# Sparse attention and expert layer on one core: second operands of VectorE in PSUM, splits of the last weights on ScalarE and VectorE, a new order

## The chip, the core and the metric

The kernel runs on one core of a Trainium2 chip. A core has five engines with instruction queues of their own: TensorE (PE, matmuls, into PSUM), VectorE (DVE), ScalarE (ACT), GpSimd (POOL) and SyncE (SP, which issues transfers). The program is one launch. The metric is the device time of that launch in microseconds, as the median of several runs. A profile is one further execution, recorded by the hardware profiler.

## The reference

The input is `q`, `k`, `v` of 8 batches, 8 heads, 576 rows and 64 features, all float32, and the weights of an expert layer.

```python
# attention: keep the scores that lie within tau of their row's maximum
scores = q @ k.T / sqrt(64)
scores = where(scores >= max(scores) - tau, scores, -1e9)
p = exp(scores - max(scores)); p /= sum(p) + 1e-9
x = (p @ v)  ->  4608 tokens of 512 features (8 heads side by side)
# expert layer: each token goes to one of 8 experts
logits = x @ w_gate + modality_bias[modality_id]
e = argmax(logits); gate = softmax(logits)[e]
out = gate * (relu(x @ w1[e]) @ w2[e])      # w1 512x1024, w2 1024x512
```

## The kernel before

**Attention.** 8 batches have 4 pairs of heads each, a pair has 9 steps of 128 score rows, 288 steps in all. A step is: PE writes 128 x 576 scores into a pair of PSUM banks (`qk`, L827); DVE takes the row maximum (`nm`, L836 and L838); ACT the exponential (`e`, L842); DVE masks and sums the row (`pr`, L854); PE transposes `pr` (L880), ACT copies the result out (L883), and PE multiplies it by `v` (L761). Since float32 products are made of rounded parts, each matmul operand is kept as a high part and the rest (`hi`, `lo`), and a product takes three matmuls. For keys and queries POOL makes these parts (`stack`, L727 and L729).

**Routing.** After the fourth pair of a batch PE computes the gate's logits (`gate`), and `route` (L990) runs on DVE: logits summed over heads (L996), their maximum (L997), its subtraction (L998), the first expert that reaches it (L1001 to L1004), a count by matmuls of how many earlier tokens each expert has (`f3`), and the place of each token in the expert's list (L1020 to L1024). `pos` keeps the running count. POOL scatters the tokens' numbers and row factors into a table in HBM (`tab`). The modality bias is prepared once on DVE (`late_constants`, L644 to L652).

**Slots.** An expert's work is done in slots of 256 to 512 tokens of one expert (`slot`, L1131). SP reads the expert and place from an integer in SBUF, loads the table's rows (`tb`) and 16 weight tiles of 256 KB (`wload`, into `raw`), POOL gathers the tokens (`xg`), `xt` scales each by its row factors (`xn`, L1182), PE transposes it, ACT and DVE make `xh` and `xl`; `wsplit` makes the two parts of each weight tile (L1219 or L1221 the high one, L1223 the low one); `l1` is the first layer (L1239, then `hh` on ACT, `hl` on DVE), `l2` the second (L1271, then `y`), and POOL writes the rows to the output with an indirect transfer (L1290). Eight side slots run beside attention or just behind it: after some batches are routed, `pick` (L1042) takes the expert with enough tokens waiting. In them the scaling and both parts of the weights are POOL's work. When all batches are routed, `pick_rest` (L1058) makes the list of the slots that are left from the counts, in some 40 small DVE instructions on one partition; three such slots are always run (`last_slot`: two of 512, one of 320 tokens; further ones under a condition). In these the scaling, the high parts (ACT) and the low parts of `w1` (DVE) are not on POOL, the low parts of `w2` are. Tiles of the last slots have names with a `t` ahead (`tw1h`, `txg`).

**The order.** Nothing is issued in the order of the text. Each step is an `op` with an engine, an assumed duration, what it reads and writes, and a due time. `SHIFTS` is a compressed table with one byte for each op that moves its due time by up to 8 us. `Plan.order` (L148) plays the engines forward with these durations: an engine that is free takes the ready op that is due first; PSUM banks are given out on the way. While attention runs, two pairs of banks belong to scores and four single banks (`bk`) to all else; afterwards all eight are single (`pm` are the four former ones). An op that names a `Group` holds its bank from its first to its last op. What comes out is the fixed order of every engine's queue. Lines of `late_constants`, `route`, `pick_rest` and `slot` are those that the change edits, beside the planner's constants.

Of the kernel before, what the change touches and what calls it, by code (L numbers as in the profile page):

```python
# [77 lines left out]
class Plan:  # L78
# [4 lines left out]
    LAND = (0.2, 1.05, 1.7, 4.5)  # L83
# [62 lines left out]
    def order(self, banks, late):  # L146
# [54 lines left out]
        def begin(e, t):  # L201
# [51 lines left out]
            for j in o.succ:  # L253
                x = ops[j]
                same = x.eng == o.eng and o.dma is None
                x.soon = max(x.soon, fin + (self.NEXT if same else self.LAT).get(o.eng, 0.0 if same else 0.04))
                x.left -= 1
                if not x.left and x.hot:
                    coming.add(j)
# [7 lines left out]
        while heap:  # L267
            t = heap[0][0]
            while heap and heap[0][0] <= t + 1e-9:
# [9 lines left out]
                else:  # L279
# [10 lines left out]
                    for j in o.succ:  # L290
                        s = ops[j]
                        same = s.eng == o.eng and o.dma is None
                        s.ready = max(s.ready, t + (self.NEXT if same else self.LAT).get(o.eng, 0.0 if same else 0.04))
# [52 lines left out]
def tile_attn_moe(  # L346
# [166 lines left out]
    pos2 = tiles(glob, 2, [P, NT + 1, NE], F32, "pos")  # L513
# [104 lines left out]
    def late_constants():  # L618
# [24 lines left out]
        def f():  # L643
            nc.vector.tensor_copy(out=mid_f[:, 1, :], in_=mid_i.rearrange("p b t two -> p (b t) two")[:, :, 0])  # L644
            nc.vector.tensor_scalar(out=mid_f[:, 0, :], in0=mid_f[:, 1, :], scalar1=0.0, scalar2=None,
                                    op0=ALU.is_equal)
        op("DVE", 0.8, f, [(bi, b) for b in range(B + 1)], [bf])
# [4 lines left out]
        op("DVE", 0.45, lambda: nc.vector.tensor_tensor(out=bias_t, in0=bias_t, in1=bias_u, op=ALU.add),  # L652
# [286 lines left out]
    def x_out(p):  # L939
# [6 lines left out]
        for a in range(KC):  # L946
# [3 lines left out]
                 src.rearrange("i k p r -> i k (p r)"), rd=[src], wr=[("xs", b, h, a)], us=0.6)  # L950
# [36 lines left out]
    def counted(nb):  # L987
        return pos2[(nb - 1) % 2][:, NT, :] if nb else creg

    def route(b):  # L990
# [3 lines left out]

        def f1():
            V.tensor_reduce(out=lt, in_=lg.rearrange("p c h e -> p c e h"), axis=AX.X, op=ALU.add)  # L996
            V.tensor_reduce(out=mx, in_=lt, axis=AX.X, op=ALU.max)  # L997
            V.tensor_tensor(out=lt, in0=lt, in1=mx.unsqueeze(2).to_broadcast(shp_t), op=ALU.subtract)  # L998

        def f2():  # L1000
            V.scalar_tensor_tensor(out=fe, in0=lt, scalar=0.0, in1=iota_m.unsqueeze(1).to_broadcast(shp_t),  # L1001
                                   op0=ALU.is_ge, op1=ALU.mult)
            V.tensor_reduce(out=mn, in_=fe, axis=AX.X, op=ALU.min)
            V.tensor_tensor(out=oh[:, 0:NT, :], in0=iota_x, in1=mn.unsqueeze(2).to_broadcast(shp_t), op=ALU.is_equal)  # L1004
        op("DVE", 1.35, f1, [lg], [lt, mx])
# [12 lines left out]
        def f4():  # L1018
            rkv = g.t[:, 0:(NT + 1) * NE].rearrange("p (t e) -> p t e", e=NE)
# [5 lines left out]
        op("DVE", 1.0, f4, [g, counted(b), oh], [pos, posf, posi])  # L1025
# [32 lines left out]
    def pick_rest():  # L1058
        left = fin["pool"].tile([1, NE], F32, name="left", bufs=1)
        nc.vector.tensor_tensor(out=left, in0=counted(B)[0:1, :], in1=nxt, op=ALU.subtract)  # L1060
        done = fin["pool"].tile([1, NE], F32, name="done", bufs=1)
        nc.vector.tensor_tensor(out=done, in0=nxt, in1=creg[0:1, :], op=ALU.subtract)
# [3 lines left out]
        for z, w in enumerate((WM, WH, 0)):  # L1066
# [4 lines left out]
        nc.vector.tensor_reduce(out=cnt[:, 1:4, :], in_=th, axis=AX.X, op=ALU.add)  # L1071

        ns = fin["pool"].tile([1, 3, NE], F32, name="ns", bufs=1)
        nc.vector.tensor_tensor(out=ns, in0=cnt[:, 1:4, :], in1=cnt[:, 0:3, :], op=ALU.subtract)
        off = fin["pool"].tile([1, 3, NE], F32, name="off", bufs=1)
        nc.vector.scalar_tensor_tensor(out=off, in0=done.unsqueeze(1).to_broadcast([1, 3, NE]),
                                       scalar=1.0 / W, in1=cnt[:, 0:3, :], op0=ALU.mult, op1=ALU.add)
        yield
        cum = fin["pool"].tile([1, 3, NE], F32, name="cum", bufs=1)
# [6 lines left out]
        nc.vector.tensor_tensor(out=off, in0=off, in1=cum, op=ALU.subtract)  # L1086
# [6 lines left out]
        ej = fin["pool"].tile([1, 3, MAXC], F32, name="ej", bufs=1)  # L1093
# [3 lines left out]
        em = fin["pool"].tile([1, 3, MAXC], F32, name="em", bufs=1)  # L1097
        nc.vector.tensor_scalar(out=em, in0=ej, scalar1=float(-NE), scalar2=None, op0=ALU.add)
        for z in range(3):
            nc.vector.tensor_tensor(out=le[:, z], in0=em[:, z].unsqueeze(2).to_broadcast(SHP),  # L1100
                                    in1=iota_m[0:1, :].unsqueeze(1).to_broadcast(SHP), op=ALU.is_equal)
            nc.vector.tensor_tensor(out=le[:, z], in0=le[:, z], in1=off[:, z:z + 1, :].to_broadcast(SHP),
                                    op=ALU.mult)
            yield
        bj = fin["pool"].tile([1, 3, MAXC], F32, name="bj", bufs=1)
# [3 lines left out]
        nc.vector.tensor_scalar(out=bj, in0=bj, scalar1=float(W), scalar2=float(W), op0=ALU.mult, op1=ALU.add)  # L1109
        nc.vector.scalar_tensor_tensor(out=bj, in0=ej, scalar=float(CAP), in1=bj, op0=ALU.mult, op1=ALU.add)  # L1110
# [19 lines left out]

    def slot(z, where, nrow, WT, rg, xt_eng, keys, late=(), hold=()):  # L1131
# [3 lines left out]
        c1 = 0.695 * WT / 512 if WT > 256 else 0.36  # L1135
# [5 lines left out]
        def expert():  # L1141
            def f():
                box["e"] = nc.values_load(where()[0], engines=[ET.SP], min_val=0, max_val=NE - 1)
            op("SP", 0.4, f, keys, [(z, "e")])

        def rows():
# [7 lines left out]
            op("SP", 0.9, f, keys + ["tab"] + [("tab", b, t) for b in range(nb) for t in range(NT)], [tb], dma=0.4)  # L1154

        def gather(t):
            def f():
# [7 lines left out]
                   [xg], dma=1.0)  # L1165
            return f

        def xt(t):
            def f():
# [27 lines left out]
        def wload(which, f_):  # L1197
            def f():
# [12 lines left out]
                op("SP", 0.42, g, late + [(z, "e")], [raw], dma=0.9)  # L1211
            return f

        def wsplit(which, f_):
            def f():
                raw = box.pop(("raw", which, f_))
                hi, lo = rg[f"w{which}h"].next(), rg[f"w{which}l"].next()
                if xt_eng:
# [3 lines left out]
                d = xt_eng and which == 1  # L1222
# [36 lines left out]
        def l2(gg, t, y):  # L1259
            def f():  # L1260
# [12 lines left out]
                op("PE", 0.695, h, [wh, wl] + [(x, i) for x in (hh, hl) for i in range(2)], [g])  # L1273
# [98 lines left out]
    for z, (w, nb) in enumerate(SIDE):  # L1372
# [11 lines left out]
        for t, f in slot(z, lambda cells=cells: cells["c"], nb * S, w, rings, False, [pk_i[z]], hold=hold)(t0, span, OPEN):  # L1384
# [13 lines left out]
    def finish():  # L1398
# [4 lines left out]
        steps = pick_rest()  # L1403
        for us in [0.6] + [0.7] * 3 + [0.8] + [0.6] * 3 + [0.9, 0.5, 0.9, 0.6, 0.6, 0.9, 0.7, 1.4, 0.7]:
            op("DVE", us, lambda: next(steps, None), ["fin", counted(B)[0:1], nxt, creg, cnt], [cnt, "si"])
# [28 lines left out]
    def idle(g, n):  # L1434
# [4 lines left out]
        c-k#iXCM^(1OA;&lvFaRH+d<QRgtnIA-i(6oITEV&Yowl<Lu+?jLx3fl7vzyTS}CfS=Qa}|9<#CAD)lTr)McYNexQ&vBBHo{d4OHHd=Oe&n%  # L1439
# [123 lines left out]
```

## Time and profile before

| | |
|---|---|
| median of 3 runs | 995.2 us (991.33 to 996.54) |
| profiled execution | 1002.75 us |
| its span, first to last instruction | 1000.9 us |
| mean granted TensorE clock | 0.988 of full |
| busy: PE, DVE, ACT, POOL | 961.2, 747.2, 614.3, 593.8 us |
| transferred | 159.6 MB, mean 159 GB/s |

Busy times are sums over an engine's instructions without overlaps; register, wait and transfer-issuing instructions are not in them. Starts of matmuls are recorded, their ends are modelled, so back-to-back matmuls overlap in the record. In the profile a line such as L1223 is the kernel's line that issued the instruction. Attention takes the first 770 us or so, the last slots end the program.

### The profile page before, as it was taken

What the parts mean: (1) busy time and instruction counts of PE and PEld (TensorE: products, weight loads), DVE (VectorE), ACT (ScalarE), POOL (GpSimd) and SP (SyncE); (2) the same over time, 40 slices, a digit from 0 to 9 for tenths busy, and PEclk for the clock granted to TensorE, in tenths of its full rate; (3) what the DMA queues carried; (4) which work ended last, traced back from release to release, by engine and by line L of the source; (5) the groups of instructions that cost most, each with busy time, mean ns of one, the idle gap of its engine ahead of it and who ended that gap; (6) DMA issues with size and microseconds to landing.
All of it is one profiled execution on the core that took longest, in us unless ns stands there. A gap on an engine that the chain in (4) does not pass through costs nothing.

```text
span 1000.9 us, 19578 instructions
## 1 busy us (share of the span) xinstructions
PE 961.2 (96%) x6304; PEld 768.8 (77%) x6304; DVE 747.2 (75%) x1792; ACT 614.3 (61%) x1256; POOL 593.8 (59%) x746
## 2 busy tenths in 40 slices
PE   7999999989999999999899999999999989899997
PEld 6776677768787877778789778877887866688886
DVE  6898888878788979878878888879785574625242
ACT  6777678667767776767577668766764233143431
POOL 3533686487378645737667575538964879823241
PEclk9999999999999999999999999999999989999999
DMA  7888989888879996897679786778753376333410
GB/s 162 167 192 183 196 189 191 169 204 185 182 140 194 191 193 128 185 183 167 148 158 200 178 171 147 179 142 186 190 136 87 97 199 200 116 104 103 142 63 28
DMA packets 310448, 159.58 MB, mean 159 GB/s; under 512 B 235902, under 2 KB 281982, under 8 KB 308416
## 3 DMA queue, kind: packets, MB, share of 16 engines
q1 hardware_dynamic: 301024, 138.64, 64.3%
q0 software_dynamic: 7200, 19.07, 6.2%
q8 instruction: 52, 0.85, 0.4%
q10 hardware_dynamic: 2112, 0.52, 0.2%
q14 instruction: 60, 0.49, 0.2%
HBM read 85.98 MB, written 20.73 MB: 107 GB/s over the span
## 4 chain that ended last, share of the span: by engine, by line
PE 48%; DVE 5%; issue 3%; POOL 2%; ACT 1%; another core or an unknown queue 0%; POOLq 0%; ACTq 0%; DVEq 0%
PE bk L1239 11%; PE bk L1271 11%; PE bk L761 7%; PE s L827 7%; PE bk L880 5%; PE pm L1271 3%; PE pm L1239 1%; PE bk L1187 1%; DVE pr L854 1%; DVE nm L836 1%; DVE xn L1182 1%; DVE le L1090 1%; PE bk L893 1%; POOL out_dram L1290 0%; PE bk L961 0%
## 5 line engine op out<-in xcount | busy, mean ns | idle before, releaser
L842 ACT ACTIVATE e<-s,nm 128x576 f32<-128x576 f32 x288 | 213.9, 746 | 73.6 <-DVE nm L836 67.9
L854 DVE SCALAR_TENSOR_TENSOR pr<-s,nm,e 128x576 f32<-128x576 f32 x288 | 231.3, 812 | 28.8 <-ACT e L842 10.2
L836 DVE TENSOR_REDUCE nm<-s 128x1 f32<-128x576 f32 x288 | 214.8, 749 | 30.7 <-PE s L827 25.3
L827 PE MATMUL s<-km,q 128*128 128x288 f32 x1024 | 190.9, 313 | 7.0 <-DVE pr L854 5.0
L883 ACT COPY ptm<-bk 128x512 f32<-128x512 f32 x256 | 146.3, 592 | 45.3 <-PE bk L880 37.0
L827 PEld LDWEIGHTS s<-km,q 128*128 128x128 f32 x1024 | 147.5, 189 | 34.4 <-DVE pr L854 14.0
L880 PE MATMUL bk<-ident,pr 128*128 128x128 f32 x1152 | 166.4, 275 | 1.4 <-DVE hl L1253 1.4
L880 PEld LDWEIGHTS bk<-ident,pr 128*128 128x128 f32 x1152 | 136.6, 141 | 19.1 <-issue 2.9
L761 PE MATMUL bk<-ptm,v_m 128*64 128x256 f32 (+1 forms) x1024 | 139.7, 417 | 2.3 <-ACT ptr L900 2.3
L761 PEld LDWEIGHTS bk<-ptm,v_m 128*64 128x64 f32 x1024 | 69.2, 138 | 53.6 <-issue 11.1
L1253 DVE SCALAR_TENSOR_TENSOR hl<-bk,hh 128x512 fp32r<-128x512 f32 (+3 forms) x78 | 45.9, 591 | 64.3 <-ACT hh L1251 64.1
L1239 PE MATMUL bk<-xh,w1h 128*128 128x512 f32 (+2 forms) x240 | 89.7, 374 | 0.2
L729 POOL TENSOR_TENSOR q<-kqt,q 128x576 fp32r<-128x576 f32 x62 | 88.0, 1423 | 2.3
L1271 PE MATMUL bk<-w2h,hh 128*128 128x512 f32 x200 | 84.7, 423 | 0.0
L1239 PE MATMUL bk<-xh,w1l 128*128 128x512 f32 (+2 forms) x240 | 83.8, 349 | 0.4 <-POOL w1l L1223 0.4
L1223 POOL TENSOR_TENSOR w1l<-raw,w1h 128x512 fp32r<-128x512 f32 x64 | 82.3, 1288 | 2.9
L1239 PE MATMUL bk<-xl,w1h 128*128 128x512 f32 (+2 forms) x240 | 83.6, 348 | 0.0
L1223 POOL TENSOR_TENSOR w2l<-raw,w2h 128x512 fp32r<-128x512 f32 x64 | 81.9, 1284 | 2.2
L1271 PE MATMUL bk<-w2l,hh 128*128 128x512 f32 x200 | 79.5, 398 | 2.0 <-POOL w2l L1223 2.0
L727 POOL CAST q<-kqt 128x576 fp32r<-128x576 f32 x62 | 41.0, 668 | 65.0 <-PE s L827 36.7
L1271 PE MATMUL bk<-w2h,hl 128*128 128x512 f32 x200 | 79.1, 396 | 0.0
L1290 POOL DMA_INDIRECT out_dram<-y,tb x37 | 38.2, 1034 | 61.8 <-DVE y L1283 46.1
(226 smaller groups left out, 1784.7 us busy)
## 6 DMA issues: line engine op xcount, KB each, us to landing
raw<-in_moe_w_dram SPq DMA_DIRECT2D x128, 256.0 KB
km<-q SPq DMA_DIRECT2D x60, 288.0 KB
q<-q SPq DMA_DIRECT2D x30, 576.0 KB
nk<-km SPq DMA_DIRECT2D x97, 144.0 KB
traw<-in_moe_w_dram SPq DMA_DIRECT2D x48, 256.0 KB
xs<-xq SPq DMA_DIRECT2D x64, 144.0 KB
v_m<-in_v_dram SPq DMA_DIRECT2D x64, 128.0 KB
kq<-in_q_dram SPq DMA_DIRECT2D x46, 144.0 KB
```

What stands on the lines that cost most here:

```text
L729: op("POOL", 1.425, lambda s=s: nc.gpsimd.tensor_tensor(out=q2[:, 1, s], in0=kqt[:, s], in1=f32(q2[:, 0, s]), op=ALU.subtract), [kqt[:, s] ...
L761: nc.tensor.matmul(out=o, lhsT=lhsT, rhs=rhs, start=start, stop=stop, skip_group_check=True)
L827: nc.tensor.matmul(out=g.t[:, hf, 0:SH], lhsT=a, rhs=x, start=(z == 0), stop=(z == len(passes) - 1))
L836: op("DVE", 0.757, lambda: nc.vector.tensor_reduce(out=nm[:, 0, x:x + 1], in_=g.t[:, :, 0:SH], axis=AX.XY, op=ALU.max, negate=True), [g], ...
L842: op("ACT", 0.747, lambda: nc.scalar.activation(out=e, in_=g.t[:, :, 0:SH], func=AF.Exp, bias=nm[:, 0, x:x + 1]), [g, nm[:, 0, x:x + 1]], ...
L854: op("DVE", 0.826, lambda: nc.vector.scalar_tensor_tensor(out=pr.rearrange("p (a x) -> p a x", a=2), in0=g.t[:, :, 0:SH], scalar=nm[:, 1, ...
L880: op("PE", 0.44, lambda: [nc.tensor.transpose(out=g.t[:, kc * P:(kc + 1) * P], in_=pr[:, kc * P:(kc + 1) * P], identity=ident) for kc in r ...
L883: op("ACT", 0.583, lambda: nc.scalar.copy(out=o, in_=g.t.rearrange("a (k p) -> a k p", p=P)), [g], [o])
L1223: op("DVE" if d else "POOL", 0.686 if d else 1.29, lambda: (nc.vector if d else nc.gpsimd).tensor_tensor(out=lo.t, in0=raw.t, in1=f32(hi.t ...
L1239: nc.tensor.matmul(out=g.t[:, 0:WT], lhsT=a.t[:, cs], rhs=x.t[:, c, 0:WT], start=(c == 0 and y == 0), stop=(c == KC - 1 and y == 2))
L1253: op("DVE", 0.1 + 0.58 * WT / 512, lambda: nc.vector.scalar_tensor_tensor(out=hl.t[:, 0:WT], in0=g.t[:, 0:WT], scalar=0.0, in1=f32(hh.t[:, ...
L1271: nc.tensor.matmul(out=g.t, lhsT=a.t[:, ts], rhs=w.t, start=(y == 0 and i == 0), stop=(y == F2 - 1 and i == 2))
```

## The change

1. In `route` the intermediate results (maximum, its comparison, the expert's number, the positions) lie in the PSUM bank that holds the count, in place of SBUF tiles; it is opened by the first instruction. One `is_ge` and one small add are new; `pos` keeps only the running count.
2. In `pick_rest` most second operands lie in one PSUM bank (`room`); two reduces over one element copy `nxt` and `cnt` there.
3. Where the scaling is DVE's, ACT copies the slot's row factors into a PSUM bank, and DVE reads them there.
4. The eighth side slot (the one that waits for all 8 batches) scales on DVE. Its weights, those of the seventh that are due after the last attention step (`OWN`), and all of the last slots have their high part made by ACT and their low part by DVE.
5. The modality bias is prepared by POOL.
6. The planner's assumed durations and its `SHIFTS` are others, so the order of all queues is another.

```diff
-    LAND = (0.2, 1.05, 1.7, 4.5)
+    LAND = (0.0, 1.0, 1.95, 4.9)
+    WAKE = 0.7
...
-            nc.vector.tensor_copy(out=mid_f[:, 1, :], in_=mid_i.rearrange("p b t two -> p (b t) two")[:, :, 0])
+            nc.gpsimd.tensor_copy(out=mid_f[:, 1, :], in_=mid_i.rearrange("p b t two -> p (b t) two")[:, :, 0])
...
-            op("DVE", 0.45, lambda m=m, t=t: nc.vector.tensor_tensor(
+            op("POOL", 0.8, lambda m=m, t=t: nc.gpsimd.tensor_tensor(
...
+        g = Group()
+        part = lambda x, n: g.t[:, x:x + n * NE].rearrange("p (t e) -> p t e", e=NE)
+        one = lambda x: g.t[:, x:x + NT]
+
         def f1():
             V.tensor_reduce(out=lt, in_=lg.rearrange("p c h e -> p c e h"), axis=AX.X, op=ALU.add)
-            V.tensor_reduce(out=mx, in_=lt, axis=AX.X, op=ALU.max)
-            V.tensor_tensor(out=lt, in0=lt, in1=mx.unsqueeze(2).to_broadcast(shp_t), op=ALU.subtract)
+            V.tensor_reduce(out=one(48), in_=lt, axis=AX.X, op=ALU.max)
+            V.tensor_tensor(out=part(64, NT), in0=lt, in1=one(48).unsqueeze(2).to_broadcast(shp_t), op=ALU.is_ge)
+            V.tensor_tensor(out=lt, in0=lt, in1=one(48).unsqueeze(2).to_broadcast(shp_t), op=ALU.subtract)
...
-            V.tensor_tensor(out=pos, in0=rkv, in1=counted(b).unsqueeze(1).to_broadcast([P, NT + 1, NE]), op=ALU.add)
-            V.tensor_tensor(out=pos[:, 0:NT, :], in0=pos[:, 0:NT, :], in1=oh[:, 0:NT, :], op=ALU.mult)
-            V.tensor_reduce(out=posf, in_=pos[:, 0:NT, :], axis=AX.X, op=ALU.add)
+            V.tensor_tensor(out=part(64, NT), in0=part(0, NT), in1=counted(b).unsqueeze(1).to_broadcast(shp_t),
+                            op=ALU.add)
+            V.tensor_tensor(out=part(104, NT), in0=part(64, NT), in1=oh[:, 0:NT, :], op=ALU.mult)
+            V.tensor_reduce(out=posf, in_=part(104, NT), axis=AX.X, op=ALU.add)
...
+            V.tensor_tensor(out=pos, in0=part(NT * NE, 1)[:, 0], in1=counted(b), op=ALU.add)
...
-        cum = fin["pool"].tile([1, 3, NE], F32, name="cum", bufs=1)
+        cum = room(3, NE)
...
-        ej = fin["pool"].tile([1, 3, MAXC], F32, name="ej", bufs=1)
+        ej = room(3, MAXC)
...
+    OWN = tm(NSTEP) + 2
...
+                if xt_eng and t == 0:
+                    box["r"] = gr = Group()
+                    op("ACT", 0.25, lambda: nc.scalar.copy(
+                        out=gr.t[:, 0:TT * H].rearrange("p (t h) -> p t h", h=H), in_=tb.t[:, 0:TT, 2:TC].bitcast(F32)),
+                       late + [tb], [gr], due=plan.due - 2)
+                r_ = lambda tb: tb.t[:, t, 2:TC].bitcast(F32)
+                if xt_eng:
+                    r_ = lambda tb, gr=box["r"]: gr.t[:, t * H:(t + 1) * H]
...
-                if xt_eng:
+                d = xt_eng or plan.due > OWN
+                if d:
                     op("ACT", 0.62, lambda: nc.scalar.copy(out=hi.t, in_=raw.t), late + [raw], [hi])
                 else:
                     op("POOL", 0.613, lambda: nc.gpsimd.tensor_copy(out=hi.t, in_=raw.t), [raw], [hi])
-                d = xt_eng and which == 1
                 op("DVE" if d else "POOL", 0.686 if d else 1.29, lambda: (nc.vector if d else nc.gpsimd).tensor_tensor(
...
-        for t, f in slot(z, lambda cells=cells: cells["c"], nb * S, w, rings, False, [pk_i[z]], hold=hold)(t0, span, OPEN):
+        for t, f in slot(z, lambda cells=cells: cells["c"], nb * S, w, rings, nb == B, [pk_i[z]], hold=hold)(t0, span, OPEN):
...
```

## Rows read from the trace of the kernel before

**Rows 1.** Busy us (instructions) by engine in four stretches: PE, PEld, DVE, ACT, POOL; PEclk, DMA, GB/s

```profile
20.00:740.00 720.00, 700.63 (x4990) 557.81 (x4987) 612.62 (x1536) 517.57 (x1074) 445.23 (x554) 0.99 0.83 176
...
800.00:820.00 20.00, 16.86 (x69) 13.13 (x68) 13.87 (x33) 5.77 (x11) 14.57 (x20) 0.83 0.57 154
...
840.00:860.00 20.00, 15.53 (x65) 11.99 (x64) 16.96 (x11) 6.72 (x11) 18.49 (x20) 0.91 0.41 118
...
880.00:900.00 20.00, 20.00 (x88) 16.19 (x87) 3.87 (x6) 8.69 (x16) 5.00 (x4) 1.00 0.29 82
```

**Rows 2.** Waits, 796 to 880 us: who waited for whom: us, times, longest

```profile
PE bk L1187 <- DVE xn L1182: 3.3, 1, 3.3
PE pm L1271 <- DVE hl L1253: 3.1, 1, 3.1
...
PE bk L1271 <- POOL w2l L1223: 2.0, 3, 0.8
...
PE bk L1239 <- POOL w1l L1223: 0.4, 1, 0.4
```

**Rows 3.** Busy times and granted clock behind the two long waits

```profile
804.00:810.00 6.00, 6.00 (x17) 4.73 (x18) 4.37 (x19) 0.59 (x1) 2.21 (x4) 0.52 0.20 47
...
854.60:858.00 3.40, 3.40 (x11) 2.92 (x12) 2.79 (x3) 0.59 (x1) 3.21 (x4) 0.57 0.42 132
```

**Rows 4.** Timeline of DVE: start, us, line, out<-in, count [idle before <-releaser]

```profile
796.42 5.63 DVE L1090 TENSOR_TENSOR le<-ij,cum 1x88 f32<-1x88 f32 x3
...
849.18 5.35 DVE L1182 TENSOR_TENSOR xn<-txg,tb 128x256 f32<-128x256 f32 x2 [0.48 <-PE bk L1187]
```

**Rows 5.** Tiles `le`, `xn`, `tw1l` and line L998: ns min/median/max, first and last start

```profile
L1090 DVE TENSOR_TENSOR le<-ij,cum x3: 707/753/4311, 796.4 to 797.7; 1x88 f32<-1x88 f32 x3
...
L1102 DVE TENSOR_TENSOR le<-le,off x3: 236/236/236, 803.1 to 804.6; 1x88 f32<-1x88 f32 x3
...
L1182 DVE TENSOR_TENSOR xn<-txg,tb x22: 413/420/4953, 842.2 to 957.4; 128x256 f32<-128x256 f32 x22
...
L1223 DVE TENSOR_TENSOR tw1l<-traw,tw1h x24: 679/683/4464, 817.2 to 978.4; 128x512 fp32r<-128x512 f32 x24
...
L998 DVE TENSOR_TENSOR l<-l,lmx x8: 199/299/2100, 101.4 to 773.5; 128x40 f32<-128x40 f32 x8
```

**Rows 6.** Timelines of POOL and DVE near 867 us

```profile
866.54 1.02 POOL L1290 DMA_INDIRECT out_dram<-y,tb  x1 [2.88 <-DVE y L1283]
...
866.85 0.75 DVE L1182 TENSOR_TENSOR xn<-txg,tb 128x256 f32<-128x256 f32 x2
```

**Rows 7.** Groups by line and shape: busy us, mean ns | idle before, releasers

```profile
L998 DVE TENSOR_TENSOR l<-l,lmx 128x40 f32<-128x40 f32 x8 | 5.7, 708 | 0.3
...
L1021 DVE TENSOR_TENSOR pos<-pos,oh 128x40 f32<-128x40 f32 x8 | 2.8, 355 | 0.3
...
L1020 DVE TENSOR_TENSOR pos<-bk,pos 128x48 f32<-128x48 f32 x7 | 1.4, 205 | 1.9 <-PE bk L761 1.9
...
L1223 POOL TENSOR_TENSOR w2l<-raw,w2h 128x512 fp32r<-128x512 f32 x64 | 81.9, 1284 | 2.2
...
L1221 POOL CAST w2h<-raw 128x512 fp32r<-128x512 f32 x64 | 39.7, 628 | 43.4 <-PE bk L1271 27.2 <-DMA raw<-in_moe_w_dram 16.1
...
L1219 ACT CAST tw2h<-traw 128x512 fp32r<-128x512 f32 x24 | 14.7, 620 | 19.3 <-PE pm L1271 12.7 <-DMA traw<-in_moe_w_dram 2.6 <-PE bk L1271 2.5
```

**Rows 8.** Modality bias: timelines of DVE and PE, then busy times of 40 to 60

```profile
46.87 1.35 DVE L644 CAST y<-xg 128x40 f32<-128x40 int32 x1 [0.73 <-DMA xg<-in_moe_modality_id_dram]
...
50.23 0.80 PE L827 MATMUL s<-km,q 128*128 128x288 f32 x4 [1.31 <-DVE pr L854]
...
40.00:60.00 20.00, 17.87 (x136) 13.77 (x135) 18.44 (x47) 14.05 (x28) 8.68 (x19) 1.00 0.81 183
```

**Rows 9.** The seventh routing: timelines of DVE and PE

```profile
682.20 0.82 DVE L996 TENSOR_REDUCE l<-lg 128x40 f32<-128x360 f32 x1
...
688.05 0.18 PE L761 MATMUL bk<-oh,ltri 128*128 128x48 bf16 x1 [0.75 <-DVE y L1283]
```

More of the change, by code (lines that the diff above doesn't have):

```diff
@@ L255, in begin @@
                 same = x.eng == o.eng and o.dma is None
[L256 removed]
+                x.soon = max(x.soon, fin + (self.NEXT if same else self.LAT).get(o.eng, 0.0 if same else 0.04)
+                                    + (self.WAKE if o.dma is not None and x.eng == "SP" else 0.0))
                 x.left -= 1
@@ L292, in order @@
                         same = s.eng == o.eng and o.dma is None
-                        s.ready = max(s.ready, t + (self.NEXT if same else self.LAT).get(o.eng, 0.0 if same else 0.04))
+                        s.ready = max(s.ready, t + (self.NEXT if same else self.LAT).get(o.eng, 0.0 if same else 0.04)
+                                        + (self.WAKE if o.dma is not None and s.eng == "SP" else 0.0))
                         s.n -= 1
@@ L484, in paced @@
         return i
+    ISSUE = {1.05: 0.7, 0.1: 0.8, 0.2: 0.75, 0.6: 0.66, 0.95: 0.72, 1.3: 0.58, 2.6: 0.56}
     def load(out, in_, rd=(), wr=(), us=1.0, due=None, eng="SP"):
         q_ = {"SP": nc.sync, "ACT": nc.scalar, "POOL": nc.gpsimd}[eng]
-        op(eng, 0.6, lambda: q_.dma_start(out=out, in_=in_), rd, list(wr) or [out], dma=us, due=due)
+        op(eng, 1.0 if eng == "POOL" else 0.5 if eng == "ACT" else ISSUE.get(us, 0.65), lambda: q_.dma_start(out=out, in_=in_), rd, list(wr) or [out], dma=us, due=due)
     warm = keep(glob, [P, 1], F32, "warm")
@@ L1058, in pick_rest, with room @@
     def pick_rest():
-        left = fin["pool"].tile([1, NE], F32, name="left", bufs=1)
-        nc.vector.tensor_tensor(out=left, in0=counted(B)[0:1, :], in1=nxt, op=ALU.subtract)
+        at_, taken = fin["ps"], [0]
+        def room(*shape):
+            n = 1
+            for x in shape:
+                n *= x
+            taken[0] += n
+            t = at_[0:1, taken[0] - n:taken[0]]
+            if len(shape) == 2:
+                return t.rearrange("o (a b) -> o a b", b=shape[1])
+            if len(shape) == 3:
+                return t.rearrange("o (a b c) -> o a b c", b=shape[1], c=shape[2])
+            return t
+        nx, left = room(NE), room(NE)
+        nc.vector.tensor_reduce(out=nx, in_=nxt.unsqueeze(2), axis=AX.X, op=ALU.add)
+        nc.vector.tensor_tensor(out=left, in0=counted(B)[0:1, :], in1=nx, op=ALU.subtract)
         done = fin["pool"].tile([1, NE], F32, name="done", bufs=1)
-        nc.vector.tensor_tensor(out=done, in0=nxt, in1=creg[0:1, :], op=ALU.subtract)
+        nc.vector.tensor_tensor(out=done, in0=nx, in1=creg[0:1, :], op=ALU.subtract)
         yield
@@ L1085, in pick_rest @@
         nc.vector.tensor_tensor(out=off, in0=off, in1=ns, op=ALU.add)
-        nc.vector.tensor_tensor(out=off, in0=off, in1=cum, op=ALU.subtract)
+        offp = room(3, NE)
+        nc.vector.tensor_tensor(out=offp, in0=off, in1=cum, op=ALU.subtract)
         SHP = [1, MAXC, NE]
@@ L1401, in finish, with step @@
         plan.ops[-1].deps |= {i for i in range(len(plan.ops) - 1) if plan.ops[i].att}
-        steps = pick_rest()
+        steps, gp = pick_rest(), Group()
+        def step():
+            fin["ps"] = gp.t
+            next(steps, None)
         for us in [0.6] + [0.7] * 3 + [0.8] + [0.6] * 3 + [0.9, 0.5, 0.9, 0.6, 0.6, 0.9, 0.7, 1.4, 0.7]:
-            op("DVE", us, lambda: next(steps, None), ["fin", counted(B)[0:1], nxt, creg, cnt], [cnt, "si"])
+            op("DVE", us, step, ["fin", counted(B)[0:1], nxt, creg, cnt], [cnt, gp, "si"])
         for b in [tail["xg"].next() for _ in range(4)]:
```

203 lines of the change are left out of this document (101 added, 102 removed).

## The prediction

> **What bounds the kernel now.** I read the views in this order. First the busy times by stretch. TensorE (PE) is the bound through most of the attention steps (700.6 of 720 us busy from 20 to 740) and again near the end (20 of 20 us from 880 to 900). Between the two lies a hole: 16.9 busy of 20 us from 800 to 820 and 15.5 of 20 from 840 to 860, while GpSimd (POOL) is busy 14.6 and 18.5 of the same 20 [rows 1]. Next the waits of 796 to 880 us, to see what ended each idle time of PE: VectorE (DVE) twice with more than 3 us, POOL's weight splits four times with less than 1 [rows 2]. [...] Last, the timeline of DVE, to see why it was late.
>
> There the reader is to see one mechanism. From 796.4 three DVE compares of 88 numbers on one partition last 5.63 us, with the `hl` that PE waits for queued behind them; at 849.18 two row scalings last 5.35 us, with PE's transposes behind them [rows 4]. The same two forms take 0.24 us (the multiply beside the compares has their shape) and 0.42 us when nothing holds them, and up to 4.3 and 5.0 us at worst [rows 5]. All of them read two tensors in SBUF, and in both stretches POOL is nearly full of splits. An indirect DMA of POOL doesn't hold DVE: with one from 866.54 to 867.56, two row scalings together took 0.75 us [rows 6]. DVE work with one operand in PSUM isn't held either: the position add reads PSUM and a small SBUF tensor and averages 205 ns over seven cases [rows 7], near its 0.2 us neighbours.
>
> **The change part by part.**
> 1. *Expert table (`pick_rest`).* Its compares get `cum` and most other second operands from PSUM. Three compares go from 5.63 us to 3 x 0.24 = 0.7 us, so `hl` isn't late any more and PE's 3.1 us go [rows 2, 4, 5]. The two copies that put an operand into PSUM (`nx`, `below`) are two more small DVE instructions, some 0.4 us, beside PE's work.
> 2. *Row factors.* ScalarE (ACT) copies them to PSUM once per slot, 0.25 us, four slots; every scaling takes 0.42 us, and PE's 3.3 us at 854.6 go [rows 2, 5]. The eighth side slot moves its eight scalings from POOL to DVE, 8 x 0.42 = 3.4 us more, beside PE's matmuls.
> 3. *Weight splits.* The 16 weights of the eighth side slot and about two thirds of the seventh's (those due after the last attention step) move from POOL (0.63 and 1.28 us each) to ACT (0.62) and DVE (0.68); of the three last slots the 24 low parts of `w2` move from POOL to DVE [rows 5, 7]. That is some 27 x 1.9 + 24 x 1.3 = 82 us off POOL, 17 us more on ACT, 51 x 0.68 = 35 us more on DVE, over some 200 us. A weight feeds 12 matmuls; at 88 matmuls in 20 us [rows 1] that is 2.7 us of PE, against 0.68 us of DVE and 0.62 of ACT: they keep ahead. PE's waits for POOL, 2.0 + 0.4 us, go [rows 2]. SyncE's loads wait for the buffer that a split frees, so they go out earlier, and POOL's gathers no longer queue behind splits.
> 4. *Clock.* With the two long waits goes the half clock behind them: 6.0 x 0.48 = 2.9 us and 3.4 x 0.43 = 1.5 us [rows 3].
>
>    Parts 1 to 4 sum to 3.1 + 3.3 + 2.4 + 4.4 = 13.2 us, the most that they can give. What is late next is PE itself, which has no holes from 880 on; I take 12.5, with a small wait left in the new order. The least is one long wait and its clock alone, 3.3 + 1.5, about 5.
> 5. *Routing.* The subtraction of the row's maximum averages 708 ns and the multiply by the one-hot 355 [rows 7]. With the second operand in PSUM I take the 205 ns of the position add for both: 8 x (0.50 + 0.15) = 5.2 us off DVE. New are an `is_ge` and an add on eight numbers, 8 x 0.35 = 2.8 us. Net 2.4 us of DVE among softmax steps, while PE mostly has side slots to do. Worth 0 to 2.4 us; I take 1.
>    [...]
> 6. *Modality bias.* Five DVE instructions go to POOL, in a stretch where DVE is busy 18.4 of 20 us and POOL 8.7. The first alone lasts 1.35 us at 46.87; with the four others (0.5 to 0.6 us each) it is 3.4 us. Shortly after it PE idles 1.31 us for DVE's `pr` [rows 8]. On POOL they take some 3 us, in its idle time; what is queued behind them there, a remainder copy of 0.24 us, is as late as that. Worth between -1 and 3.4 us; I take 2, since DVE is the bound there.
> 7. *New order.* Other planner costs and another table of shifts reorder every engine and with it every queue, SyncE's and POOL's too. It computes nothing more or less. PE's gaps of 20 to 740 us come to 19.4 us [rows 1], the most that it could give back. I take 0, with 8 either way.
>
> Sum: 12.5 + 1 + 2 = 15.5 us. The profiled execution took 1002.75 us (span 1000.9 and 1.85 around it), 0.8% above the median of the runs, 995.2, and above the highest of them; the holes belong to the program, so I take the 15.5 us from both: 987 for a profiled execution, **980** for the median.
>
> **The rivals.**
> - *A: DVE stays held* (0.15). The 51 low parts that come to DVE read two tensors in SBUF and can be held as `tw1l` was, once for 4.46 us [rows 5]. For it: POOL keeps the rest of the seventh slot's splits. Against it: behind those POOL has hardly more than indirect DMAs and short memsets, and the former hold nothing [rows 6]. If the waits move from `xn` to the splits, part 1, its clock, and parts 5 and 6 at their lower half remain: 3.1 + 2.9 + 2 = 8 us, 987 us. [...]
> - *B: the order gives more* (0.10). It closes 12 of the 19.4 us of gaps in attention: 968 us.
> - *C: slower, through a PSUM bank* (0.06). The routing's bank is now opened by its first instruction and held until the positions are read. In the seventh routing the first instruction (`l`) starts at 682.20, the matmuls that now open the bank at 688.05 [rows 9]: 5.9 us more. There are four single banks in attention, for transposes, value products and the side slots' sums. If a side slot can't open its bank and PE loses half of those 5.9 us, eight routings cost 24 us against the gain of 15.5: 1004 us. It decides from 2.6 us per routing. Against it: the order is laid out with the banks counted, and other work stands ready.
> - *D: the order costs what the tail gives* (0.07). PE's gaps in attention grow from 19 to some 35 us: 996 us, no change.
>
> The forecast itself, 974 to 986 us, has 0.62.
>
> **How the numbers follow.** About 0.5% (5 us) is what a measurement of this kernel can tell from no change: faster is below 990.2, slower above 1000.2. Faster: 0.62, B's 0.10 and 0.10 of A's 0.15, together 0.82. Same: 0.05 of A and D's 0.07, 0.12. Slower: C, 0.06. The range leaves out no more than 2 in 10: from 968 (half of B) to 992 (nearly all of A), without C and D.
>
> **What would show it.** Right: compares of 0.2 to 0.3 us; all DVE row scalings near 0.42; no wait of PE over 1 us between the end of attention and the last 15 us, with a granted clock near 1.00 there; POOL busy less than half of 800 to 860; five DVE instructions fewer near 50 us. Wrong: PE waiting for a low part or for `xn` in the tail (A), or idle around the routings (C); a last score later than before by more than some us (D). The number fails most easily through the order, for which no row stands.

## The result, and the profile after

The changed kernel takes **984.3 us** (median; 979.9 to 985.7), the kernel before 995.5 us beside it: a ratio of 0.989, 95% interval 0.985 to 0.993, some 11 us faster. Beside the later experiments it was timed again, with 0.9891 (0.9855 to 0.9928). The profiled execution has a span of 984.0 us, 16.9 us shorter than that of before.

The stretches of [rows 1] in the trace after (busy us and instructions of PE, PEld, DVE, ACT, POOL; granted PE clock, DMA share, GB/s):

```profile
20.00:740.00 720.00, 706.81 (x5014) 560.13 (x5016) 609.80 (x1550) 517.12 (x1079) 449.26 (x562) 0.99 0.83 177
...
800.00:820.00 20.00, 20.00 (x95) 16.52 (x95) 16.12 (x41) 7.67 (x15) 6.05 (x6) 1.00 0.56 154
840.00:860.00 20.00, 20.00 (x97) 16.51 (x96) 11.77 (x23) 6.94 (x14) 7.14 (x7) 1.00 0.50 163
880.00:900.00 20.00, 20.00 (x96) 16.33 (x95) 12.29 (x23) 8.41 (x15) 4.20 (x4) 1.00 0.41 122
```

The hole is gone. PE is full from 800 to 975 with the clock at 1.00, and POOL fell from 14.6 and 18.5 us to 6.1 and 7.1. The list of PE's waits from 755 us to the end, which held those of [rows 2], is empty. The forms of [rows 5], by line (ns min/median/max, first and last start):

```profile
L1115 DVE TENSOR_TENSOR le<-ij,bk x3: 226/227/234, 796.4 to 796.7; 1x88 f32<-1x88 f32 x3
...
L1219 DVE TENSOR_TENSOR xn<-txg,bk x16: 411/414/422, 822.3 to 893.6; 128x256 f32<-128x256 f32 x16
...
L1260 DVE TENSOR_TENSOR tw1l<-traw,tw1h x24: 676/683/693, 823.0 to 955.0; 128x512 fp32r<-128x512 f32 x24
...
L1005 DVE TENSOR_TENSOR l<-l,bk x8: 195/195/197, 104.6 to 771.8; 128x40 f32<-128x40 f32 x8
```

None of these is held any more. But `tw1l` still reads two tensors in SBUF, and it too came down, from 4464 ns at worst to 693. That is the first hint that the operand in PSUM is not what freed DVE here.

To see where the 16.9 us come from, the last score matmul splits the span (line of the scores, the tile with the last start; first the trace of before, then after):

```profile
L827 PE MATMUL s<-nk,qb x192: 290/295/402, 26.1 to 755.5; 128*128 128x288 f32 x192
```

```profile
L829 PE MATMUL s<-nk,qb x192: 290/294/403, 28.4 to 754.5; 128*128 128x288 f32 x192
```

In front of it attention gained 1.0 us. Behind it lie 1000.9 - 755.5 = 245.4 us before and 984.0 - 754.5 = 229.5 after: the tail gave 15.9. Some 1.6 of them are the order's: it leaves 1079 matmuls behind the last score (1080 in e1's profile) where the order before left 1087, at 0.21 us each (95 in 20 us). The tail repeats well (229.5 to 230.1 us in six profiles of five kernels with PSUM or SBUF operands, below); the start of the last score does not (754.5 and 759.6 in two profiles of the same changed kernel). So tails are compared by profile, everything else by timed ratio.

The longest hold that is left lies in attention. DVE and POOL near 694 us, start, duration, operation:

```profile
693.84 0.58 DVE L1060 TENSOR_TENSOR nxt<-nxt,pk 1x8 f32<-1x8 f32 x1
...
694.52 3.08 DVE L1063 CAST pk_i<-pk 1x2 int32<-1x2 f32 x1
697.52 1.42 DVE L719 STREAM_TRANSPOSE kqt<-kq 128x576 f32<-128x576 f32 x2
```

```profile
694.42 0.62 POOL L1259 CAST w2h<-raw 128x512 fp32r<-128x512 f32 x1
695.00 2.51 POOL L1260 TENSOR_TENSOR w2l<-raw,w2h 128x512 fp32r<-128x512 f32 x2
697.45 0.62 POOL L1259 CAST w1h<-raw 128x512 fp32r<-128x512 f32 x1
```

A cast of two numbers lasts 3.08 us and ends 0.1 us behind the third of the POOL splits beside it; all eight casts have a median of 0.16. The key transposes are queued behind it, and PE waits 1.9 us at 700 for what follows them.

### The profile page after: what moved, and what is told of

It is laid out like the page before. It is cut to its first block, busy times and chain, and to the rows that moved or that the text cites. A ratio compares the mean times of both kernels' runs of the same rounds, so it can differ in the third digit from the quotient of the medians.

```text
span 984.0 us, 19624 instructions
## 1 busy us (share of the span) xinstructions
PE 959.8 (98%) x6316; PEld 767.4 (78%) x6316; DVE 751.0 (76%) x1862; ACT 625.1 (64%) x1285; POOL 512.6 (52%) x669
## 4 chain that ended last, share of the span: by engine, by line
PE 67%; DVE 4%; POOL 3%; issue 2%; ACT 1%; DMA 0%; POOLq 0%; DVEq 0%
PE bk L1276 15%; PE bk L1308 14%; PE s L829 11%; PE bk L763 10%; PE bk L882 7%; PE pm L1308 3%; PE pm L1276 2%; PE bk L1224 1%; PE bk L895 1%; DVE pr L856 1%; DVE nm L838 1%; PE bk L963 1%; POOL w2l L1260 1%; POOL tab L1041 0%; POOL out_dram L1327 0%
## 5 line engine op out<-in xcount | busy, mean ns | idle before, releaser
L856 DVE SCALAR_TENSOR_TENSOR pr<-s,nm,e 128x576 f32<-128x576 f32 x288 | 232.2, 813 | 28.5 <-ACT e L844 17.6
L763 PE MATMUL bk<-ptm,v_m 128*64 128x256 f32 (+1 forms) x1024 | 137.6, 413 | 0.5 <-DMA v_m<-in_v_dram 0.4
L1276 PE MATMUL bk<-xh,w1h 128*128 128x512 f32 (+2 forms) x244 | 92.1, 377 | 0.2
L1308 PE MATMUL bk<-w2h,hh 128*128 128x512 f32 x192 | 82.4, 429 | 0.2 <-POOL w2h L1259 0.2
L871 ACT COPY rp<-pr 128x64 f32<-128x64 f32 x234 | 57.1, 254 | 34.7 <-DVE pr L856 33.6
L1308 PE MATMUL bk<-w2l,hh 128*128 128x512 f32 x192 | 76.0, 396 | 0.8 <-POOL w2l L1260 0.8
L1308 PE MATMUL bk<-w2h,hl 128*128 128x512 f32 x192 | 76.1, 396 | 0.0
L1260 POOL TENSOR_TENSOR w1l<-raw,w1h 128x512 fp32r<-128x512 f32 x52 | 66.7, 1285 | 2.5
L1260 POOL TENSOR_TENSOR w2l<-raw,w2h 128x512 fp32r<-128x512 f32 x51 | 65.2, 1284 | 2.0
```

What stands on the lines that cost most here:

```text
L763: nc.tensor.matmul(out=o, lhsT=lhsT, rhs=rhs, start=start, stop=stop, skip_group_check=True)
L856: op("DVE", 0.826, lambda: nc.vector.scalar_tensor_tensor(out=pr.rearrange("p (a x) -> p a x", a=2), in0=g.t[:, :, 0:SH], scalar=nm[:, 1, ...
L871: op("ACT", 0.248, lambda: nc.scalar.copy(out=o, in_=i), [i], [o])
L1260: op("DVE" if d else "POOL", 0.686 if d else 1.29, lambda: (nc.vector if d else nc.gpsimd).tensor_tensor(out=lo.t, in0=raw.t, in1=f32(hi.t ...
L1276: nc.tensor.matmul(out=g.t[:, 0:WT], lhsT=a.t[:, cs], rhs=x.t[:, c, 0:WT], start=(c == 0 and y == 0), stop=(c == KC - 1 and y == 2))
L1308: nc.tensor.matmul(out=g.t, lhsT=a.t[:, ts], rhs=w.t, start=(y == 0 and i == 0), stop=(y == F2 - 1 and i == 2))
```

## The experiments

Theory: a DVE instruction that reads two SBUF tensors, or copies within SBUF, is held while POOL works through splits; either an operand in PSUM or an empty POOL frees it. Rival: the new order carries the gain. All ratios are to the kernel before, timed beside it on the same chip, with 95% intervals. "Tail" is the span of the profile less the start of its last score matmul.

| run | edit | ratio | tail, us |
|---|---|---|---|
| after | the change | 0.9888 (0.9846 to 0.9930) | 229.5 |
| e1 | the change again | 0.9891 (0.9855 to 0.9928) | 229.9 |
| e2 | its casts as `tensor_scalar` | 0.9878 (0.9838 to 0.9917) | 230.1 |
| e3 | its order, operands, splits and bias put back | 1.0110 (1.0072 to 1.0148) | 242.2 |
| e4 | kernel before, only the splits moved | 0.9846 (0.9809 to 0.9883) | 231.1 |
| e5 | the change, row factors, routing, table in SBUF | 0.9996 (0.9979 to 1.0013) | 230.0 |
| e6 | the change, splits back on POOL | 0.9966 (0.9950 to 0.9982) | 238.0 |
| e7 | the change, bias back on DVE | 0.9917 (0.9888 to 0.9946) | 232.6 |
| e9 | the change, row factors and table in SBUF | 0.9874 (0.9855 to 0.9893) | 229.9 |
| e10 | the change, pick and position in PSUM | 0.9848 (0.9829 to 0.9867) | 230.0 |
| e11 | e4 with routing and pick in PSUM, eighth slot's scaling on DVE | 0.9879 (0.9856 to 0.9903) | 232.0 |
| e12 | e10, bias back on DVE | 0.9848 (0.9833 to 0.9863) | 232.2 |

In e3 and e6 the eighth slot's scaling stays on DVE. The 2 to 3 us that the tails of e7 and e12 have over the change's lie behind PE's last matmul (10.1 and 9.7 us to the end of the span, 7.1 in the change); why is not known.

**e1, e3 and e4: order or parts?** e3 and e4 keep the queues' order of the kernel that they start from; only the engine or the memory changes.

> The changed kernel once more, beside the next three on the same chip, so that small differences between them can be read. Both theories: about 11 us under the kernel before (984 against 995).

> The changed kernel in its own order of instructions, but with all placements put back: row factors, routing and expert table read SBUF, the splits of slots seven and eight are GpSimd's again, the low parts of w2 of the last slots too, the modality bias is VectorE's. Theory (the parts carry the gain, the order about nothing): 995 to 1000 us, with VectorE instructions of 3 to 5 us again between 780 and 880 and TensorE waiting 2 to 3 us behind them. Rival (the order carries it): 983 to 988 us.

> The other direction: the kernel before in its own order, with only the weight splits moved as in the change (slots seven and eight to ScalarE and VectorE, low parts of w2 of the last slots to VectorE); row factors and expert table stay in SBUF. Theory (VectorE is held only while GpSimd is nearly full): the holds of 5.6 and 5.4 us go without any operand in PSUM, 13.2 us of terms 1 to 4 come: 982 to 985 us. Rival 1 (PSUM operands are needed): two-operand instructions in SBUF still last 3 to 5 us, 990 to 995 us. Rival 2 (the order carries it): 994 to 996 us.

```
# e4, in wsplit of the kernel before
+ own = xt_eng or nb_ == B or plan.due > tm(NSTEP) + 2
- nc.gpsimd.tensor_copy(out=hi.t, ...)
+ (nc.scalar.copy if own else nc.gpsimd.tensor_copy)(out=hi.t, ...)
- (nc.vector if d else nc.gpsimd).tensor_tensor(out=lo.t, ...)
+ (nc.vector if d or own else nc.gpsimd).tensor_tensor(out=lo.t, ...)
```

e3 came out worse than the theory allowed: 1.011, 11 us slower than before, with `xn` and `tw1l` at 2.2 and 2.4 us at most and not at 3 to 5. So the parts carry the gain, and the new order without them loses. e4 took the whole of the expected gain with no operand in PSUM: 0.9846, some 15 us. Its busy times, and its scaling and compares, which read SBUF as before:

```profile
800.00:880.00 80.00, 79.76 (x364) 65.14 (x364) 46.74 (x89) 34.01 (x60) 24.07 (x25) 1.00 0.58 179
```

```profile
L1183 DVE TENSOR_TENSOR xn<-txg,tb x22: 411/418/461, 833.9 to 941.9; 128x256 f32<-128x256 f32 x22
...
L1090 DVE TENSOR_TENSOR le<-ij,cum x3: 229/232/1433, 795.4 to 797.0; 1x88 f32<-1x88 f32 x3
```

POOL is down to 24 of 80 us (64 before), no scaling lasts over 0.46, one compare is still held for 1.4 us, and the tail is 231.1. Rival 1 of e4 falls: in the tail, with POOL mostly free, SBUF operands are hardly held.

**e5, e6 and e9: which operand, and what without the splits?**

> The changed kernel with row factors, routing and expert table read from SBUF again; the weight splits stay on ScalarE and VectorE, the order stays. Theory A (with GpSimd nearly idle behind attention nothing holds VectorE, so the PSUM operands are a second lock on the same door): the time of the changed kernel, within 2 us, plus up to 1 us for the routing; row scalings 0.42 us. Theory B (each part gives its own term): 6 to 12 us slower, scalings of 3 to 5 us and half clock behind them.

> The changed kernel with only the weight splits put back to GpSimd (slots seven and eight whole, low parts of w2 in the last slots); row factors, routing and expert table keep their operand in PSUM. Theory A (the PSUM operands alone free VectorE from the hold): scalings 0.42 and compares 0.24 us, no wait of TensorE over 2 us for either, but GpSimd's splits are late: 2.4 us to 6 us over the changed kernel. Rival (GpSimd as the bound of 780 to 880 us): the waits for xn and hl are gone, those for low parts are longer, 10 us or more over the changed kernel.

> The changed kernel with row factors and expert table read from SBUF, routing still from PSUM, splits still off GpSimd. Theory (behind attention the moved splits alone do it, and the 9 us of the run with all three put back were the routing's): the time of the changed kernel within 2 us, last score near 755 us, 230 us from there to the end. Rival (the 9 us came from row factors or expert table, through the order): 993 to 996 us.

```
# e9 (and e5), xt: the factors stay in tb
- if xt_eng:
-     r_ = lambda tb, gr=box["r"]: gr.t[:, t * H:(t + 1) * H]
# e9 (and e5), the expert table
- fin["ps"] = gp.t
+ if "ps" not in fin: fin["ps"] = fin["pool"].tile([1, 512], F32, ...)
# e5 alone, route; rts is a tile in SBUF
- part = lambda x, n: g.t[:, x:x + n * NE]...
+ part = lambda x, n: (rts[:, x - 56:] if 64 <= x else g.t[:, x:])[:, 0:n * NE]...
# e6, wsplit: own are slots seven and eight, low also w2 of the last slots
+ (nc.gpsimd.tensor_copy if own else nc.scalar.copy)(out=hi.t, ...)
+ (nc.vector if d and not low else nc.gpsimd).tensor_tensor(out=lo.t, ...)
```

I expected e5 near the changed kernel, or slow through its tail. It is slow, 0.9996, but its tail is 230.0: both theories missed the place. e9, which keeps only the routing in PSUM, is as fast as the change (0.9874). So row factors and expert table in PSUM are worth nothing once the splits are moved, and the routing's operands are worth (0.9996 - 0.9874) x 995 = 12 us in this order. How it comes about, in e5: three groups of the routing (busy us, mean ns), then PE's longest waits from 20 to 975 us:

```profile
L1005 DVE TENSOR_TENSOR rts<-l,rts 128x40 f32<-128x40 f32 x8 | 5.0, 620 | 0.3
...
L1029 DVE TENSOR_TENSOR rts<-rts,oh 128x40 f32<-128x40 f32 x8 | 4.6, 570 | 0.3
L1012 DVE TENSOR_TENSOR oh<-iota_x,rts 128x40 bf16<-128x40 f32 x8 | 4.1, 517 | 0.3
```

```profile
PE s L830 <- DVE pr L857: 3.9, 8, 0.9
PE bk L883 <- ACT ot L931: 3.7, 1, 3.7
PE bk L764 <- DVE oh L1012: 3.4, 5, 1.6
```

In the changed kernel the same three average 204, 207 and 195 ns, `pr` stands with 1.8 us and `oh` does not appear. The planner of the change assumes 1.6 and 0.7 us for the routing's first two steps, the planner of before 1.35 and 1.87: the new order puts PE's count matmuls close behind a routing that is not held, and pays for one that is. e5's last score starts at 764.0 us, e9's at 754.2. The waits that e5's list has over e9's at the routing and behind DVE (`oh` 3.4, `pos` 1.7, `pr` 2.1 more, `ot` 1.8 more) come to 9.0 of these 9.8 us.

e6 is the rival's case in kind, not in size. With POOL's splits back the scalings keep 0.41 us and the compares 0.23, as in the change; PE waits for POOL instead (waits of 780 to 900 us):

```profile
PE bk L1278 <- POOL w1l L1262: 2.8, 4, 1.1
PE bk L1310 <- POOL w2l L1262: 1.7, 1, 1.7
PE bk L1278 <- POOL w1h L1259: 1.2, 1, 1.2
```

Tail 238.0, 8 us over the change. So the PSUM operands do free what carries them, but PE then waits for POOL's own splits, and `tw1l`, with both operands in SBUF, averages 0.96 us there and is held again. By time e6 lies (0.9966 - 0.9888) x 995 = 8 us over the change, between the ranges of theory A and of the rival.

Four kernels of the same order now tell the two edits apart in the tail: neither 242.2 us (e3), operands alone 238.0 (e6), splits alone 230.0 (e5), both 229.5 (the change). The operands give 4.2 us without the moved splits and 0.5 with them; the splits give 12.2 and 8.5.

**e8: the hold by itself.**

> Nothing of the reference is computed (the output is filled with zeros). Eight times each of eleven VectorE forms, first with GpSimd idle, then beside back-to-back GpSimd subtractions of 128x512, then beside its copies, then beside its memsets. Theory (a VectorE instruction with two SBUF tensors, and a copy or cast, waits for a pause of GpSimd): the first tensor_tensor with two SBUF operands lasts as long as GpSimd's run of 6 (some 7 us), copy and cast likewise; tensor_tensor with an operand in PSUM, tensor_scalar, tensor_reduce and transpose keep 0.1 to 0.8 us; beside memsets nothing is held. Rival (every VectorE access to SBUF is slowed a little while GpSimd works): all forms 1.2 to 2 times as long, none over 2 us.

Timeline of DVE, each group of eight instructions as one: first alone (three rows), then beside six POOL subtractions of 128x512 (7.96 us in a row), then beside POOL memsets:

```profile
3.56 1.83 DVE L381 TENSOR_TENSOR o<-x,y 128x40 f32<-128x40 f32 x8
5.78 1.80 DVE L382 TENSOR_TENSOR o<-x,pp 128x40 f32<-128x40 f32 x8
14.47 1.71 DVE L386 CAST oi<-x 128x40 int32<-128x40 f32 x8
...
37.79 8.42 DVE L381 TENSOR_TENSOR o<-x,y 128x40 f32<-128x40 f32 x8
46.53 1.80 DVE L382 TENSOR_TENSOR o<-x,pp 128x40 f32<-128x40 f32 x8
54.49 8.42 DVE L383 SCALAR_TENSOR_TENSOR o<-x,y 128x40 f32<-128x40 f32 x8
63.24 1.82 DVE L384 SCALAR_TENSOR_TENSOR o<-pp,y 128x40 f32<-128x40 f32 x8
79.39 5.60 DVE L386 CAST oi<-x 128x40 int32<-128x40 f32 x8
87.59 5.59 DVE L387 TENSOR_SCALAR o<-x 128x40 f32<-128x40 f32 x8
95.79 1.80 DVE L388 TENSOR_REDUCE r<-x 128x5 f32<-128x40 f32 x8
...
223.51 1.82 DVE L381 TENSOR_TENSOR o<-x,y 128x40 f32<-128x40 f32 x8
270.04 4.55 DVE L386 CAST oi<-x 128x40 int32<-128x40 f32 x8
```

Held are the forms that the theory named, with two corrections; how long is another matter. With two SBUF tensors eight instructions take 8.42 us instead of 1.83. With one of the two in PSUM (`pp`), second or first, they take 1.80 and 1.82, as when alone, and are never held. Reductions (1.80) and transposes of 128x576 (6.46) also take what they take alone. The first correction: `tensor_scalar` is held like the cast (5.59 and 5.60, each 1.71 alone), so e2's substitute was none. The second: beside memsets two SBUF operands are free (1.82), while casts are held (4.55), and with them copies and `tensor_scalar`: each of the three forms averages 506 ns over its 32 instructions in the bench. Beside POOL's copies (0.63 us on average) all the forms that the subtractions hold are held too (5.29 or 5.30 us for eight).

The theory expected one hold of some 7 us. The single durations beside the subtractions show many short ones (ns min/median/max, two SBUF tensors, then copies):

```profile
L381 DVE TENSOR_TENSOR o<-x,y x8: 199/1304/1307, 37.8 to 46.0; 128x40 f32<-128x40 f32 x8
L385 DVE COPY o<-x x8: 184/654/1237, 71.2 to 76.6; 128x40 f32<-128x40 f32 x8
```

Six of the eight wait for one subtraction each (1.26 us) and end 0.06 us behind it; the last two run free. Of the copies half are held, for 1.24 us at most. In the kernel a hold outlasted the POOL instruction that it met. The third compare of before starts at 797.74 and lasts 4.31 us [rows 5], beside five POOL instructions:

```profile
797.65 0.64 POOL L1221 CAST w1h<-raw 128x512 fp32r<-128x512 f32 x1
798.26 1.28 POOL L1223 TENSOR_TENSOR w2l<-raw,w2h 128x512 fp32r<-128x512 f32 x1
799.51 1.29 POOL L1223 TENSOR_TENSOR w1l<-raw,w1h 128x512 fp32r<-128x512 f32 x1
800.77 1.19 POOL L1182 TENSOR_TENSOR xn<-xg,tb 128x256 f32<-128x256 f32 x2
```

In the bench POOL's subtractions start 0.08 us behind the end of the one ahead, in the kernel some 0.03 us in front of it. Whether that gap is what frees DVE was not tested, and it can't be all: the cast at 694 ended although POOL's next cast had begun without a gap (697.45).

POOL is slowed in turn. Beside eight DVE subtractions of 128x512 with two SBUF tensors, which take 5.77 us alone, its six take 9.60 us instead of 7.96:

```profile
103.77 9.60 POOL L395 TENSOR_TENSOR go<-gx,gy 128x512 f32<-128x512 f32 x6
103.83 11.54 DVE L389 TENSOR_TENSOR bo<-bx,by 128x512 f32<-128x512 f32 x8
```

**e2 and e10: the last hold.**

> The changed kernel with the two float-to-int casts (row to fetch, position) written as tensor_scalar with an add of 0; nothing else moves. Theory (a VectorE cast or a two-operand tensor_tensor in SBUF is held while GpSimd works through splits, a tensor_scalar is not): no instance of the row cast over 0.3 us (now once 3.08 us at 694.5), the wait of TensorE near 700 us of 1.85 us and the half clock behind it go, 2 to 4 us under the changed kernel run beside it. Rival (the cast stood late for another reason, for instance a slow write of an integer): the new instruction lasts 3 us in the same place and the time is that of the changed kernel.

> The changed kernel with the expert pick's operands and the position before its cast in spare columns of PSUM (two small instructions more per pick), so that nothing in the pick reads two SBUF tensors or copies from SBUF to SBUF. Theory (what is left of the holds sits there: 3.1 us once near 694, 0.2 to 1 us in other picks and position casts): no instruction of the pick over 0.3 us, the wait of TensorE for ot near 700 us under 1 us, 2 to 5 us under the changed kernel. Rival (TensorE near 700 us waits for something else, the hold only sits beside it): no difference in time.

```
# e2
- nc.vector.tensor_copy(out=si, in_=r)
+ nc.vector.tensor_scalar(out=si, in0=r, scalar1=0.0, scalar2=None, op0=ALU.add)
# e10, pick (all but the last); nx, a, rp_ are spare columns of a score bank
+ nc.vector.tensor_reduce(out=nx, in_=nxt.unsqueeze(2), axis=AX.X, op=ALU.add)
+ nc.vector.tensor_tensor(out=a, in0=counted(nb)[0:1, :], in1=nx, op=ALU.subtract)
...
- nc.vector.tensor_copy(out=si, in_=r)
+ nc.vector.tensor_copy(out=si, in_=rp_)
# e10, route: the position goes through PSUM
- V.tensor_copy(out=posi, in_=posf)
+ V.tensor_copy(out=posi, in_=one(152))
```

e2 gained nothing: 0.9878, no different from e1 beside it. The hold moved to the neighbour, which reads two SBUF tensors (timeline of DVE in e2):

```profile
693.47 0.67 DVE L1058 TENSOR_SCALAR pk<-iota_m,pk 1x8 f32<-1x8 f32 x1
694.17 3.13 DVE L1060 TENSOR_TENSOR nxt<-nxt,pk 1x8 f32<-1x8 f32 x1
697.24 0.13 DVE L1061 TENSOR_SCALAR pk<-pk 1x1 f32<-1x1 f32 x1
```

In e10 nothing of the pick is left to hold (min/median/max):

```profile
L1083 DVE TENSOR_TENSOR nxt<-nxt,s x7: 151/151/151, 109.0 to 689.0; 1x8 f32<-1x8 f32 x7
...
L1087 DVE CAST pk_i<-s x7: 147/147/147, 109.6 to 689.6; 1x2 int32<-1x2 f32 x7
...
L1031 DVE CAST posi<-bk x8: 164/165/166, 107.5 to 766.3; 128x5 int32<-128x5 f32 x8
```

PE's wait for `ot` near 700 us is gone from its list. The time is 979.7 us (977.8 to 981.1) beside 982.6 (981.5 to 985.9) of e9 on the same chip, 0.9848: the fastest version that keeps the change's order, about 3 us. Against the change itself, which was not timed beside it, the intervals still touch, so the 3 us are likely and not shown.

**e11: the old order with all holds out.**

> The kernel before in its own order, with the splits moved, the eighth slot's row scaling on VectorE, and routing and pick with their second operands in spare columns of PSUM; expert table, row factors and modality bias as before. Theory (the holds are what costs, the new order gives nothing of its own): attention shorter by up to 9 us against the run with the splits alone, 230 us behind the last score, 973 to 982 us, below the changed kernel. Rival (the new order is needed to make use of a shorter routing): 981 to 985 us, as with the splits alone.

```
# e11, route of the kernel before; one() and pt() are spare columns of a score bank
- V.tensor_reduce(out=mx, in_=lt, axis=AX.X, op=ALU.max)
+ V.tensor_reduce(out=one(0), in_=lt, axis=AX.X, op=ALU.max)
...
# the eighth slot's scaling
+ nc.vector if nb_ == B else nc.gpsimd
```

The rival was right by time: 0.9879, not better than e4's 0.9846 (intervals overlap). The routing's instructions are short here too (`l<-l,s` averages 196 ns), yet nothing of it can be measured in the time. That an order laid out for a slow routing can't use a short one is one reading. PE's waits of 20 to 760 us name another:

```profile
PE s L827 <- DVE pos L1029: 2.3, 3, 1.4
...
PE bk L692 <- DVE s L1082: 2.0, 1, 2.0
```

The scores wait 3.1 us for the routing (`pos`, and 0.8 for `oh`), a transposition of keys 2.0 for the pick; e4's list has none of these. e11's routing and pick lie in spare columns of the score banks; whether the scores wait for those columns was not tested.

**e7 and e12: the bias.**

> The changed kernel with the five instructions of the modality bias back on VectorE. By the prediction's term: 2 us slower (between 1 faster and 3.4 slower), the time lost between 45 and 60 us. Rival (the stretch has slack): no difference.

> The kernel of the run before the last (pick and position from PSUM) with the five instructions of the modality bias back on VectorE, since the first trial of this term showed no difference and its place, 40 to 60 us, lies before everything else. By the prediction's term: 2 us slower than that kernel (ratio to the kernel before 0.987 against 0.985). Rival (the stretch has slack): 0.985, no difference.

```
- nc.gpsimd.tensor_copy(out=mid_f[:, 1, :], ...)     # and four more
+ nc.vector.tensor_copy(out=mid_f[:, 1, :], ...)
```

e7 is 0.9917 against 0.9888 and 0.9891, e12 equals e10 at 0.9848. No difference shows; e7 alone would leave room for the 2 us. In 40 to 60 us the changed kernel has PE busy 19.3 us and e7 17.9, but e10 has 18.8 and e12 18.9: the stretch itself shows no gain that repeats.

## Why the prediction was right in sum and wrong in its terms

The forecast was 980 us with 974 to 986 for the main case; 984.3 came. The reading of the bottleneck stands: two engines, one hold, POOL's splits behind it, and behind the two long waits a granted clock of 0.52 and 0.57 [rows 3]. Point by point:

- **Parts 1 to 4**, taken at 12.5 us: the tail gave 15.9 us by profile, and e4, which has these parts' splits alone, 15 us by ratio. The size was nearly right, the assignment was not. The prediction gave 3.1 and 3.3 us (and the clock behind them) to the operands in PSUM and 2.4 to the moved splits. e9 shows that the operands of row factors and table add nothing once POOL is free, e4 that the splits alone bring all of it, e3 and e6 that the operands without the moved splits bring 4.2 us of the tail. The step that failed: each edit was priced as if it removed its own wait, though both removed the same cause.
- **Part 5, routing**, taken at 1 (0 to 2.4): 12 us in the new order (e9 against e5), nothing that shows in the old (e11 against e4). The price came from the mean durations of two instructions alone. It left out the one-hot itself (`oh`, L1004), which fell from 554 ns to 195, and that PE's count matmuls in the new order stand right behind it.
- **Part 7, order**, taken at 0 with 8 either way: e5 and e4 differ in the order (and in the bias, the eighth slot's scaling and a few small instructions) and lie (0.9996 - 0.9846) x 995 = 15 us apart. With the old routing the new order loses 15, outside the bound, and e3 with all parts put back lost 11; the routing's 12 pay most of that back. The two errors cancelled, which is why the sum came out: 15 - 15 + 12 is the measured 11 within what these ratios can tell. That 984 lies so near 980 is luck in these two terms.
- **Part 6, bias**, taken at 2: no difference shown (e7, e12).
- **Rivals.** A did not come: no low part on DVE lasts over 0.7 us. B did not. C did not: among PE's waits of 20 to 975 us none is at a routing. D was half right, the order does cost as much as the tail gives, but only with the routing that the change replaced.
- **What would show it**: short compares and scalings, no wait over 1 us, clock 1.00, POOL below half of 800 to 860, all came. D's sign can't be told: the last score starts 1.0 us earlier than before in one profile of the change and 4.1 later in the other. The signs that came fit the wrong assignment just as well; only undoing one part at a time told them apart.

Left open: which of the two readings explains e11, what ends a hold, and whether a fresh order for the kernel of e4 with the holds of e10 out would go below 980 us. A new table of due times was not tried.

## What to carry to other kernels

When two edits remove the same wait, price the cause once and ask what each is worth with the other in place; here moving the splits off POOL was enough in the tail. A planned order and the durations that it was planned for are one change: neither may be judged, or kept, without the other. And where DVE shares a stretch with POOL's arithmetic, give its small instructions an operand in PSUM or make them reductions: beside POOL's subtractions in e8 eight such took 1.80 us, with two SBUF tensors 8.42. Replacing one held form by another left the hold in place in e2 (3.13 us, 3.08 in the change).

## What the hardware showed that was not expected

- A hold outlasted the POOL instruction that it met: 4.31 us for one compare beside five of them in the kernel before, 3.08 for a cast of two numbers beside three splits in the changed one. Beside subtractions that stand 0.08 us apart, in e8, it did not: no instruction of 128x40 lasted over 1.31 us.
- Copies, casts and `tensor_scalar` in SBUF were held in e8 even by POOL's memsets (4.55 us for eight, 1.71 alone), forms that read two SBUF tensors were not (1.82).
